# One core, long convolution and gated feed-forward: a new order of work, batched reciprocal roots, residual through the matmul, first loads on SyncE

## The chip, the cores and the metric

One core of a Trainium2 chip runs the whole program. The metric is the device time of one execution in microseconds (us). The kernel before took 297.24 us, the median of 8 runs from 296.48 to 297.85. Engines: PE is TensorE, DVE is VectorE, ACT is ScalarE, POOL is GpSimd, SP is SyncE, which here only issues DMAs.

## The reference, cut to what matters

```python
def _A_ref(q, k, v, shift_k, ssm_k, ssm_D):          # S = 2048, D = 640, 4 taps
    k_shift = sum of k_pad[:, t:t + S, :] * shift_k[:, ks - 1 - t]
    kv = k_shift * v
    y = irfft(rfft(kv, 2 * S) * rfft(ssm_k, 2 * S))[:S]   # long causal convolution
    y = y + kv * ssm_D
    return q * y

def _B_ref(x, w_gate, w_up, w_down):                 # F = 1728
    return (silu(x @ w_gate) * (x @ w_up)) @ w_down

x = A_q
h = x + _A_ref(_layernorm(x), A_k, A_v, A_shift_k, A_ssm_k, A_ssm_D)
h2 = h + _B_ref(_layernorm(h), B_w_gate, B_w_up, B_w_down)
```

The layernorm divides by the root of the variance plus 1e-5 and has no learned scale. All inputs and the output are bf16.

## The kernel before, in words

The 2048 rows are cut into 4 blocks n of 512 rows, and a block into 4 tiles q of 128 rows. The long convolution is done by blocks: each block of kv and each block of the convolution kernel is transformed by matmuls with cosine and sine matrices of length 1024, the transforms are multiplied elementwise and summed for every pair of blocks that adds to an output block, and a matmul brings the sum back.

The stages, with their lines in the kernel before:

- *Kernel blocks* (`gload`, `g_transform`): ssm_k block p is brought in transposed, blocks 0 and 1 by PE transposes (L334) and a copy on ACT (L338), blocks 2 and 3 by a transposing DMA (L323). It is then transformed by PE (L361) and copied to SBUF by ACT (L364).
- *kv* (`front_first` for block 0, `front_tile` for the others): block 0 multiplies k by the four taps on DVE (L395) and shifts by matmuls with banded matrices out of `perm` (L405); the other blocks load k four times, shifted, and do it on DVE (L378 to L381). `front` then folds each block into a sum and a difference of its halves, one half mirrored (L429 to L433), so that the transforms are half as long.
- *x transform* (L443, copies L448), *products* (`pair`, L453: each pair is 8 or 6 elementwise operations of 2,560 elements per partition on DVE).
- *Inverse* (`inverse`): matmuls with WI (L550), copies on ACT (L554), the mirrored half by matmuls with a flip matrix (L574), multiplication by the layernormed q (L566, L567, L577), the sum into x (L578), the second layernorm, and a transposing DMA of the result into hT (L582).
- *Layernorm* (`ln`, `scale`): per tile ACT makes the mean (L520) and the sum of squares (L521); POOL makes the variance plus eps (L524) and raises it to the power -0.5 (L525), on one column each; DVE scales the tile (L532), into xln for the first layernorm and into hl for the second. The second layernorm of block 0 takes its statistics on DVE (L516, L517).
- *Feed-forward* (`ffn`): 14 chunks c of 128 columns (the last has 64) of gate and up by PE (L618), SiLU and a copy on ACT (L623, L630), their product on DVE into tT (L632), which is the condition for ACT to write sg and uc again and so for PE's two psF buffers; then four down tiles of 28 matmuls (L644) whose last chunk uses 64 rows, the residual added on DVE from PSUM (L652), and a store by SP.

The order of the work is not written out. Every operation is handed to a planner (`Plan.add`) with its engine, an assumed duration, a priority `pr`, an earliest time `t0`, and what it reads and writes. `Plan.order` places the operations one by one, per engine, the ready one with the best priority, and repeats this up to `ROUNDS` times with priorities from a pass backwards. The result is one fixed list per engine, and each engine works its list in order. `psA` and `psF` are two PSUM tiles each; front, x transform and inverse use psA, kernel transforms and feed-forward psF. DMAs are issued by SP's list and, at the start, ACT's. At the start ACT's list loads the taps (wrow), v of block 0, perm, ssm_D, and later WG, WX, x of block 0 and WI; SP's loads k of block 0, then ssm_k blocks 0 and 1.

Of the kernel before, what the change touches and what calls it, by code (L numbers as in the profile page):

```python
# [16 lines left out]
D = 640  # L17
# [37 lines left out]
class Plan:  # L55
# [3 lines left out]
    def __init__(self, pools):  # L59
        self.ops, self.writer, self.readers = [], {}, {}  # L60
        self.pools, self.held = pools, {}

    def add(self, eng, dur, fn, r=(), w=(), pr=0, acq=None, rel=None, kb=0, after=(), t0=0.0):
        deps = set()
        for k in r:
            if k in self.writer:
                deps.add(self.writer[k])
        for k in list(w) + list(after):
            if k in self.writer:
                deps.add(self.writer[k])  # L70
            deps |= self.readers.get(k, set())
        i = len(self.ops)
        self.ops.append(dict(eng=eng, dur=dur, fn=fn, deps=deps, pr=pr, acq=acq and acq[0], rel=rel and rel[0], group=(acq or rel or (0, 0))[1], kb=kb, w=list(w), t0=t0))
        for k in r:
            self.readers.setdefault(k, set()).add(i)
        for k in w:
            self.writer[k], self.readers[k] = i, set()
        return i
# [42 lines left out]
    def forward(self, rank):  # L121
# [15 lines left out]
        while len(out) < n:  # L137
# [44 lines left out]
            for u in users[i]:  # L182
                lag = LAG.get(e, 0.12) if ops[u]["eng"] != e or o["kb"] else 0.12 if e == "DVE" else 0.0
                at[u] = max(at[u], done + lag)
# [6 lines left out]
ROUNDS = 3  # L191
# [3 lines left out]
MOVE = "add"  # L195
RES, XACT, VEC, TRANS = (), (), True, {2: 28, 3: 28}
# [11 lines left out]
def kernel(  # L208
# [33 lines left out]
    WI_h = nc.inline_tensor(make_basis()[2], name="const_wi")  # L242
    J_h = nc.inline_tensor(make_flip(), name="const_flip")
# [16 lines left out]
    kch = [tT[:, 2560 * i:2560 * (i + 1)].rearrange("p (a b) -> p a b", a=5) for i in range(2)]  # L260
# [9 lines left out]
    xln = [tl(f"xln{i}", [P, D]) for i in range(2)]  # L270
# [3 lines left out]
    y = [tl(f"y{i}", [P, D]) for i in range(2)]  # L274
    hl = [tl(f"hl{i}", [P, D]) for i in range(2)]
    drow = xln[0][0:1, :]
# [5 lines left out]
    junk = tl("junk", [P, D])  # L282
    mhalf = tl("mhalf", [P, 1], FP32)
    bn = [tl(f"bn{i}", [P, 2, 6], FP32) for i in range(2)]
    sm = {}
    smt = tl("sm", [P, NB * 8, 8], FP32)
    for n in range(NB):
        for q in range(4):
            for s in (1, 2):
                sm[n, q, s] = smt[:, 8 * n + 2 * q + s - 1, :]  # L290

    WG = last[:].rearrange("p a b -> p (a b)")[:, 0:4096].rearrange("p (a b) -> p a b", a=4)
    gT = [wd[:, 0:4, :], wd[:, 4:8, :], wd[:, 8:12, :], hT[1][:].rearrange("p a b -> p (a b)").rearrange("p (a b) -> p a b", a=4)]

# [14 lines left out]

    def load(q, dst, src, w, pr, kb, r=(), dur=0.45, after=(), t0=0.0):  # L310
        eng = {"SP": nc.sync, "ACT": nc.scalar, "POOL": nc.gpsimd}[q]
        add(q, dur, lambda: eng.dma_start(out=dst, in_=src), r=r, w=w, pr=pr, kb=kb, after=after, t0=t0)


    add("POOL", 0.1, lambda: nc.gpsimd.memset(ones[:], 1.0), w=["ones"], pr=-99)
    add("POOL", 0.1, lambda: nc.gpsimd.memset(mhalf[:], -0.5), w=["mhalf"], pr=-9)
    load("ACT", wrow, A_shift_k.partition_broadcast(1).rearrange("o a b -> o (a b)"), ["wrow"], -100, 5)
    add("ACT", 1.5, lambda: nc.scalar.activation(sg[0][0:1, 0:P], ones[:], ACT.Silu), r=["ones"], w=["sg0"], pr=-50)
    load("ACT", drow, A_ssm_D.partition_broadcast(1), ["drow"], -95.5, 5)

    def gload(p, pr, q="SP"):
# [5 lines left out]
        for kt in range(4):  # L327
            g = ("F", "T", p, kt)

            def mm(g=g, kt=kt):  # L330
# [6 lines left out]
            add("PE", 0.45, mm, r=["flip", f"kch{p % 2}"] + (["drow"] if p == 0 and kt == 0 else []), w=[g], pr=pr + 50, acq=("F", g))  # L337
            add("ACT", act(D), lambda g=g, kt=kt: nc.scalar.copy(gT[p][:, kt, :], ps(g).rearrange("p a b -> p (a b)")[:, 0:D]),  # L338
                r=[g], w=[f"gT{p}"], pr=pr - 40, rel=("F", g))
# [11 lines left out]
    for t in range(4):  # L351
        wcast(t)

    def g_transform(p, pr):
        for ct in range(NCT):
            g = ("F", "G", p, ct)

            def mm(g=g, ct=ct):
                for kt in range(4):
                    for h in range(2):  # L360
                        nc.tensor.matmul(ps(g)[:, h, 0:NH], WG[:, kt, ct * P:(ct + 1) * P],  # L361
                                         gT[p][:, kt, h * NH:(h + 1) * NH], start=(kt == 0), stop=(kt == 3))
            add("PE", 8 * 0.137, mm, r=["WG0", "WG1", f"gT{p}"], w=[g], pr=pr, acq=("F", g))
            add("ACT", act(D), lambda g=g, ct=ct: nc.scalar.copy(r3(G[p][ct // 4][:, ct % 4, :]), ps(g)[:, :, 0:NH]),  # L364
                r=[g], w=[Gk[p] + "cs"[ct // 4]], pr=pr - 900, rel=("F", g))
# [4 lines left out]

    def front_tile(n, q, pr):
# [7 lines left out]
        add("DVE", dve(2 * D), lambda: nc.vector.tensor_add(kd[:, 0:2, :], kd[:, 0:2, :], kd[:, 2:4, :]), r=ks, w=[kn], pr=pr)  # L379
# [7 lines left out]
    def first_loads():  # L387
        load("SP", kfirst[:], kk[0:MB, :].rearrange("(m p) d -> p m d", p=P), ["x1_0", "x1_1", "x1_2", "x1_3"], -98, 640)
        load("ACT", hT[0][:].rearrange("p a b -> p (a b)").rearrange("p (a b) -> p a b", a=4), vv[0:MB, :].rearrange("(m p) d -> p m d", p=P), ["v0all"], -96, 640)
        load("ACT", WG, WG_h.ap(), ["WG0", "WG1"], -95, 1024)  # L390

    def front_first(q, pr):
# [15 lines left out]
        if turn:  # L408
# [6 lines left out]
            add("ACT", act(D), lambda: nc.scalar.copy(r3(y[q][:]), ps(gv)[:, :, 0:NH]), r=[gv], w=[f"y{q}"], pr=pr - 60, rel=("F", gv))  # L415
            add("DVE", dve(D, True), lambda: nc.vector.tensor_mul(r3(rev[:, m, :]), ps(g)[:, :, 0:NH], r3(y[q][:])), r=[g, f"y{q}"], w=["rev"], pr=pr, rel=("A", g))
        else:
            add("DVE", dve(D, True), lambda: nc.vector.tensor_mul(r3(kv[:, q, :]), ps(g)[:, :, 0:NH], r3(v)), r=[g, "v0all"], w=[f"kv{q}"], pr=pr, rel=("A", g))

    def front(n, pr):  # L420
# [13 lines left out]

    def x_transform(n, pr):
# [20 lines left out]

    def hbuild(p, pr):
# [3 lines left out]

    def pair(j, p, pr, how):
# [43 lines left out]
    def ln(n, q, which, pr, vec=False, t0=0.0):  # L506

        s, k, src = sm[n, q, which], f"sm{n}{q}{which}", xin[n % 2][:, q, :]
        xk = f"x{n % 2}_{q}"
        e = nc.gpsimd  # L510
        if vec:
# [6 lines left out]
            add("DVE", 1.1, bns, r=[xk], w=[k + "a", f"bn{q % 2}"], pr=pr)  # L518
        else:
            add("ACT", act(D) + 0.25, lambda: nc.scalar.activation(junk[:], src, ACT.Copy, scale=-1.0 / D, accum_out=s[:, 0:1]), r=[xk], w=[k + "a"], pr=pr, t0=t0)  # L520
            add("ACT", act(D) + 0.45, lambda: nc.scalar.activation(junk[:], src, ACT.Square, bias=s[:, 0:1], accum_out=s[:, 1:2]), r=[xk, k + "a"], w=[k + "b"], pr=pr)  # L521

        def fin():
            e.tensor_scalar(s[:, 3:4], s[:, 1:2], 1.0 if vec else 1.0 / D, EPS, op0=ALU.mult, op1=ALU.add)  # L524
            e.tensor_tensor(s[:, 4:5], s[:, 3:4], mhalf[:], op=ALU.pow)  # L525
            if which == 1 and n in XACT:
                e.tensor_tensor(s[:, 5:6], s[:, 0:1], s[:, 4:5], op=ALU.mult)
        add("POOL", 1.5 + 0.7 * (which == 1 and n in XACT), fin, r=[k + "a", k + "b"], w=[k], pr=pr)

    def scale(dst, n, q, which):  # L530
        s = sm[n, q, which]
        nc.vector.tensor_scalar(dst, xin[n % 2][:, q, :], s[:, 0:1], s[:, 4:5],  # L532
                                op0=ALU.subtract if (n, which) == (0, 2) and VEC else ALU.add, op1=ALU.mult)

    def load_x(n, pr, queue="SP"):
        load(queue, xin[n % 2][:], xq[n * MB:(n + 1) * MB, :].rearrange("(m p) d -> p m d", p=P), [f"x{n % 2}_{q}" for q in range(4)], pr, 640, t0=(14, 30, 0, 0)[n])
        for q in range(4):
            ln(n, q, 1, pr + 30, t0=(26, 50, 0, 0)[n])

    def inverse(n, pr):  # L540
        a, ak = A[n], Ak[n]
        x, b = xin[n % 2], n % 2
        for m in range(2):
# [11 lines left out]
            for half in (0, 1):  # L555
                q = 2 + m if half == 0 else 1 - m
                yb, yk, lk = y[half], f"y{half}", f"xln{half}"
                xk = f"x{b}_{q}"
                s = sm[n, q, 1]
                if n in XACT:  # L560
                    add("ACT", act(D), lambda q=q, half=half, s=s: nc.scalar.activation(xln[half][:], x[:, q, :], ACT.Identity, scale=s[:, 4:5], bias=s[:, 5:6]),
                        r=[f"sm{n}{q}1", xk], w=[lk], pr=pr)
# [166 lines left out]
```

## Time and profile before

| what | value |
|---|---|
| median of the runs | 297.24 us |
| the profiled execution | 297.03 us |
| its span, first to last instruction | 295.2 us |
| ACT, largest groups | SiLU L623 x56 33.7 us; copies L630 x56 33.1; squares L521 x28 23.7; kernel transform copies L364 x32 21.8; means L520 x28 20.9 |
| POOL | L525 x32 35.1 us, mean 1,097 ns; L524 x32 30.7 us, mean 960 ns |
| DVE, products L453 | 115 us in 78 operations of about 1,480 ns each |
| PE, largest groups | L618 133.8 us in 540 matmuls; L644 64.8 us in 448; L361 37.6 us in 256 |
| DMA | 44.13 MB, mean 149 GB/s |

The busy times of PE are those of single matmuls and overlap; the time from start to start is shorter than the duration. The granted clock of TensorE was 0.999 of full speed over the span. A row of the timeline has the start, the length, engine, line, operation, operands, the count, and in brackets the idle time of the engine before it and what ended it. In the chain of waits each piece is what the next one waited for.

### The profile page before, as it was taken

The numbers are of one execution on the slowest core, as the hardware profiler recorded it, in microseconds if no ns is written. First come the engines' busy times: TensorE is split into PE (matmuls) and PEld (weight loads), VectorE is DVE, ScalarE is ACT, GpSimd is POOL, SyncE is SP. The second block draws the span as 40 slices with busy tenths as digits, with TensorE's granted clock in tenths as the row PEclk, the third lists the DMA queues.
The fourth block names the chain that finished last, engine by engine and source line by source line (L and its number), as shares of the span: only waits on it lengthen the run. The fifth ranks groups of instructions, "written<-read, shape, count | busy, mean of one in ns | idle before, by whom it ended". The sixth has DMA issues, their size and how long they took to land.

```text
span 295.2 us, 4406 instructions
## 1 busy us (share of the span) xinstructions
PE 275.5 (93%) x1651; PEld 157.9 (53%) x1651; DVE 229.7 (78%) x301; ACT 169.6 (57%) x323; POOL 66.2 (22%) x70
## 2 busy tenths in 40 slices
PE   3598959999999989999999999999998999999995
PEld 1266737666645535564545565555445665444563
DVE  0559797999999999999999999999999931211211
ACT  5117895898856589004996790169955732555300
POOL 0000262395000056000362174008800220000000
PEclk9999999999999999999999999999999999999999
DMA  7982399508635677934676394163654151654011
GB/s 230 392 270 88 119 238 348 121 2 245 212 91 131 178 234 160 258 131 115 169 230 206 65 192 95 44 200 91 152 130 102 42 127 54 174 139 110 0 47 46
DMA packets 67898, 44.13 MB, mean 149 GB/s; under 512 B 25442, under 2 KB 65955, under 8 KB 67748
## 3 DMA queue, kind: packets, MB, share of 16 engines
q1 hardware_dynamic: 66240, 40.23, 49.8%
q10 hardware_dynamic: 1636, 3.61, 3.4%
q8 instruction: 13, 0.21, 0.3%
q14 instruction: 9, 0.07, 0.1%
HBM read 37.28 MB, written 2.62 MB: 135 GB/s over the span
## 4 chain that ended last, share of the span: by engine, by line
DVE 52%; PE 30%; issue 5%; DMA 4%; ACT 4%; POOL 3%; ACTq 0%; DVEq 0%
DVE s L453 20%; DVE T L453 13%; PE psF L644 11%; PE psF L618 10%; DVE tT L632 3%; DVE k L378 3%; DMA perm<-const_flip 3%; PE psA L405 3%; POOL sm L525 2%; DVE k L379 2%; PE psF L361 2%; PE psA L550 2%; PE psA L443 2%; DMA hT<-hl 1%; DVE o L652 1%
## 5 line engine op out<-in xcount | busy, mean ns | idle before, releaser
L618 PE MATMUL psF<-hT,wg 128*128 128x512 bf16 x280 | 69.4, 379 | 0.8 <-ACT uc L630 0.8
L524 POOL TENSOR_SCALAR sm<-sm 128x1 f32<-128x1 f32 x32 | 30.7, 960 | 169.9 <-ACT junk L521 159.4
L644 PE MATMUL psF<-wd,tT 128*128 128x320 bf16 x448 | 64.8, 299 | 1.1 <-DVE tT L632 0.9
L618 PE MATMUL psF<-hT,wu 128*128 128x512 bf16 x260 | 64.4, 379 | 0.4 <-DMA wu<-in_B_w_up_dram 0.4
L623 ACT ACTIVATE sg<-psF 128x512 bf16<-128x512 f32 (+1 forms) x56 | 33.7, 602 | 45.7 <-PE psF L618 36.4
L644 PEld LDWEIGHTS <-tT 128*128 128x128 bf16 x448 | 41.4, 97 | 24.1 <-issue 6.9
L453 DVE TENSOR_TENSOR T<-s,s 128x2560 bf16<-128x2560 bf16 x32 | 47.2, 1481 | 0.0
L453 DVE TENSOR_TENSOR s<-s,T 128x2560 bf16<-128x2560 bf16 x32 | 47.1, 1481 | 0.0
L618 PEld LDWEIGHTS <-wg 128*128 128x128 bf16 x280 | 27.2, 98 | 32.7 <-issue 2.3
L630 ACT CAST uc<-psF 128x512 bf16<-128x512 f32 (+1 forms) x56 | 33.1, 591 | 15.8 <-PE psF L618 15.6
L632 DVE TENSOR_TENSOR tT<-sg,uc 128x512 bf16<-128x512 bf16 (+1 forms) x56 | 23.2, 418 | 24.4 <-ACT uc L630 24.4
L618 PEld LDWEIGHTS <-wu 128*128 128x128 bf16 x260 | 25.4, 98 | 29.5 <-DMA wu<-in_B_w_up_dram 0.8
L525 POOL TENSOR_TENSOR sm<-sm,mhalf 128x1 f32<-128x1 f32 x32 | 35.1, 1097 | 2.7
L361 PEld LDWEIGHTS <-s 128*128 128x128 bf16 x256 | 25.0, 98 | 11.8 <-issue 2.1
L361 PE MATMUL psF<-wd,s 128*128 128x320 bf16 x192 | 28.4, 299 | 0.9 <-ACT wd L338 0.5
L652 DVE TENSOR_TENSOR o<-psF,x 128x640 bf16<-128x640 f32 x16 | 13.1, 817 | 19.3 <-PE psF L644 19.3
L364 ACT CAST s<-psF 128x640 bf16<-128x640 f32 x32 | 21.8, 693 | 7.7 <-PE psF L361 7.6
L521 ACT ACTIVATE junk<-x,sm 128x640 bf16<-128x640 bf16 x28 | 23.7, 846 | 0.3
L520 ACT ACTIVATE junk<-x 128x640 bf16<-128x640 bf16 x28 | 20.9, 745 | 3.7 <-DVE x L578 2.9
L550 PE MATMUL psA<-s,WI 128*128 128x320 bf16 x128 | 18.9, 299 | 2.9 <-DVE s L453 2.8
L453 DVE TENSOR_TENSOR s<-s,s 128x2560 bf16<-128x2560 bf16 x14 | 20.5, 1479 | 1.2 <-ACT s L364 1.2
L443 PE MATMUL psA<-kv,WX 128*128 128x320 bf16 x128 | 20.5, 299 | 0.0
(55 smaller groups left out, 231.7 us busy)
## 6 DMA issues: line engine op xcount, KB each, us to landing
k<-in_A_k_dram SPq DMA_DIRECT2D x12, 640.0 KB, 4.8
wg<-in_B_w_gate_dram SPq DMA_DIRECT2D x24, 320.0 KB, 3.2
wu<-in_B_w_up_dram SPq DMA_DIRECT2D x24, 320.0 KB, 3.7
out_dram<-o SPq DMA_DIRECT2D x16, 160.0 KB, 1.9
wd<-in_B_w_down_dram SPq DMA_DIRECT2D x1, 2080.0 KB, 10.6
v<-in_A_v_dram SPq DMA_DIRECT2D x12, 160.0 KB, 4.7
x<-in_A_q_dram SPq DMA_DIRECT2D x3, 640.0 KB, 5.3
tT<-in_A_ssm_k_dram SPq DMA_DIRECT2D x2, 640.0 KB, 10.1
```

The costliest lines, as they stand in the source:

```text
L361: nc.tensor.matmul(ps(g)[:, h, 0:NH], WG[:, kt, ct * P:(ct + 1) * P], gT[p][:, kt, h * NH:(h + 1) * NH], start=(kt == 0), stop=(kt == 3))
L443: nc.tensor.matmul(ps(g)[:, h, 0:NH], WX[:, kt, ct * P:(ct + 1) * P], kv[:, base + kt, h * NH:(h + 1) * NH], start=(kt == 0), stop=(kt == 1))
L453: add("DVE", dve(n * D), lambda: f(o, a, b), r=ks(ak) + ks(bk), w=ks(ok), after=["WG0", "WG1"] if ok[:2] == "s7" else [], pr=pr)
L521: add("ACT", act(D) + 0.45, lambda: nc.scalar.activation(junk[:], src, ACT.Square, bias=s[:, 0:1], accum_out=s[:, 1:2]), r=[xk, k + "a"], ...
L524: e.tensor_scalar(s[:, 3:4], s[:, 1:2], 1.0 if vec else 1.0 / D, EPS, op0=ALU.mult, op1=ALU.add)
L525: e.tensor_tensor(s[:, 4:5], s[:, 3:4], mhalf[:], op=ALU.pow)
L550: nc.tensor.matmul(ps(g)[:, h, 0:NH], WI[:, 4 * part + ct, m * P:(m + 1) * P], a[part][:, ct, h * NH:(h + 1) * NH], start=(ct == 0), stop= ...
L618: i = nc.tensor.matmul(ps(gr)[:, which, :], w[:, kt, cc * P:(cc + 1) * P], hT[b][:, kt, :], start=(kt == 0), stop=(kt == 4))
L623: apart(gr, 0, nc.scalar.activation(sg[s][:z, :], ps(gr)[:z, 0, :], ACT.Silu))
L630: add("ACT", act(MB), lambda gr=gr, s=s, z=z, merged=merged: nc.scalar.copy(uc[s][:z, :], ps(gr)[64:128, 0, :] if merged else ps(gr)[:, 1, ...
L632: add("DVE", dve(MB), lambda c=c, s=s, z=z: TM(tT[:z, c * MB:(c + 1) * MB], sg[s][:z, :], uc[s][:z, :]), r=[f"sg{s}", f"uc{s}"], w=[f"tT{c ...
L644: nc.tensor.matmul(ps(gr)[:, h, 0:NH], tT[:z, c * MB + m * P:c * MB + (m + 1) * P], wd[:z, c, h * NH:(h + 1) * NH], start=(c == 0 and n no ...
```

## The change

It has these parts. The function names are those of the diff.

1. *Order.* `ROUNDS` is 0: one pass of the planner, whose priorities are shifted per stage by a table (`URGENCY`) and whose starts are held back by another (`EARLIEST`); a decorator gives each stage its name. All four engines' lists differ from before nearly everywhere.
2. *Loads.* v of block 0, ssm_D, WX, x of block 0 and WI move from ACT's list to SP's; ACT keeps the taps, perm and WG. In the list that results SP begins with one ssm_k block (block 1), then k and v of block 0, ssm_D, WX, ssm_k block 0, x of block 0, WI and then k and v of block 1. wd, before one load of 2,080 KB and one of 80, becomes five, each issued after a tT chunk is written.
3. *Warm-up.* Eight matmuls of 512 columns on zeros, five at the very start and three after the tap broadcast.
4. *Layernorm.* ACT also makes variance times 1/D plus eps (a third ACT operation on one column); POOL does a single power, for 1, 2 or 4 tiles at once (15 operations in place of 64); ahead of a batch DVE does a small `tensor_reduce` over 96 elements (`port`, 11 in all), nine of them reading the tile that ACT's Square writes; for the first layernorms of blocks 1 to 3 DVE also copies one element of the power's result (`idle`), and so waits for it.
5. *First scale of blocks 1 to 3* on ACT (12 tiles; a one-column operation for the bias and the scale itself) in place of DVE.
6. *Residual* of blocks 0 to 2: two matmuls of 320 columns with the identity per down tile, then a copy on ACT in place of DVE's add. Block 3 keeps the add.
7. *Down matmuls* use 128 rows for the last chunk as well; the unused rows of tT and wd are set to zero once.

Parts that other settings of the same code could use (rows fetched by index, a transposed way back, DMA accumulation) are switched off by `HOW = 'JJJJ'`, `TURN`, `ACC` and `MOVES`.

```diff
-        i = len(self.ops)
+        i, pr = len(self.ops), pr + URGENCY.get(self.stage or "none", 0)
+        t0 = max(t0, EARLIEST.get(self.stage or "none", 0))
...
-ROUNDS = 3
+ROUNDS = 0
-RES, XACT, VEC, TRANS = (), (), True, {2: 28, 3: 28}
+RES = (0, 1, 2)
+XACT = [(n, 1) for n in (1, 2, 3)]
+VEC = (0,)
+SPAN = 96
+HOW = 'JJJJ'
+TRANS = {2: 28, 3: 28}
+WARM = (0.43, 5, 3)
...
+    add("DVE", 0.35, lambda: nc.vector.memset(junk[:], 0.0), w=["hl0"], pr=-999)
+    add("DVE", 0.35, lambda: nc.vector.memset(tT[64:128, 13 * MB:], 0.0), w=["tz"], pr=-998)
+    add("DVE", 0.35, lambda: nc.vector.memset(wd[64:128, 13, :], 0.0), w=["wz"], pr=-998)
+    def warm(name, n, pr, r=()):
+        g = ("F", name)
+        def mm():
+            for i in range(n):
+                nc.tensor.matmul(ps(g)[:, i % 2, :], junk[:, 0:P], junk[:, 0:MB], start=True, stop=True)
...
-    load("ACT", drow, A_ssm_D.partition_broadcast(1), ["drow"], -95.5, 5)
+    load("SP", drow, A_ssm_D.partition_broadcast(1), ["drow"], -95.5, 5)
...
+            def spread():
+                nc.scalar.activation(junks[j][:], src, ACT.Square, bias=s[:, 0:1], accum_out=s[:, 1:2])
+                nc.scalar.activation(var[:, c:c + 1], s[:, 1:2], ACT.Identity, scale=1.0 / D, bias=eps[:])
+    def port(key, deps, pr, lag, src=None):
+        src = still if src is None else src
+        add("DVE", 0.06 + SPAN / 960, lambda: nc.vector.tensor_reduce(idle[:], src[:, 0:SPAN], axis=mybir.AxisListType.X, op=ALU.add), r=deps, w=[key], pr=pr, lag=lag)
+    def root(n, qs, which, pr):
+        cs, vec = sorted(column(n, q, which) for q in qs), which == 2 and n in VEC
+        gap, gk, lag = (still, "flip", 0.3) if vec else (junks[qs[-1] % 2], f"junk{qs[-1] % 2}", 0.0)
...
+        if n < NB - 1 or which == 1:
+            gkey = [ks[0] + "g"]
+            port(gkey[0], deps + [gk], pr - 20000, lag, gap)
+        add("POOL", 0.8, lambda: nc.gpsimd.tensor_tensor(rstd[:, c0:c1], var[:, c0:c1], mhalf[:, 0:c1 - c0], op=ALU.pow), r=deps + gkey, w=ks, pr=pr)
+        if (n, which) in XACT:
+            add("DVE", 0.08, lambda: nc.vector.tensor_copy(idle[:], rstd[:, c0:c0 + 1]), r=ks, w=[ks[0] + "h"], pr=pr - 20000)
...
+        def on_act():
+            nc.scalar.activation(s[:, 2:3], s[:, 0:1], ACT.Copy, scale=r)
+            nc.scalar.activation(dst, src, ACT.Identity, scale=r, bias=s[:, 2:3])
...
-                        z = 64 if c == 13 else P
                         for h in range(2):
-                            nc.tensor.matmul(ps(gr)[:, h, 0:NH], tT[:z, c * MB + m * P:c * MB + (m + 1) * P],
-                                             wd[:z, c, h * NH:(h + 1) * NH], start=(c == 0 and n not in RES), stop=(c == 13))
+                            nc.tensor.matmul(ps(gr)[:, h, 0:NH], tT[:, c * MB + m * P:c * MB + (m + 1) * P],
+                                             wd[:, c, h * NH:(h + 1) * NH], start=(c == 0 and not res), stop=(c == 13))
...
-    load_x(0, -10, "ACT")
+    load_x(0, -10, "SP")
-    load("ACT", WI[:], WI_h.ap(), ["WI"], -5, 512, t0=16)
+    load("SP", WI[:], WI_h.ap(), ["WI"], -5, 512, t0=16)
...
+            load("SP", wd[:, c0:c1, :], B_w_down[c0 * P:c1 * P, :].rearrange("(kt p) d -> p kt d", p=P), [f"wd{i}"], 1200, 160 * (c1 - c0),
+                 r=[f"tT{2 * min(i, 2) + 1}"], after=["gT0", "gT1", "gT2"])
```

## The prediction

> **What bounds it.** I read the page from the shares down to the chain, then the chain's last part, then VectorE's and PE's rows in order of time. First the page: busy shares, the 40 slices, the chain by engine.
>
> ```profile
> PE 275.5 (93%) x1651; PEld 157.9 (53%) x1651; DVE 229.7 (78%) x301; ACT 169.6 (57%) x323; POOL 66.2 (22%) x70
> PE   3598959999999989999999999999998999999995
> DVE  0559797999999999999999999999999931211211
> DVE 52%; PE 30%; issue 5%; DMA 4%; ACT 4%; POOL 3%; ACTq 0%; DVEq 0%
> ```
>
> VectorE (DVE) is full from about 24 us to 227 us and nearly idle afterwards; PE is full throughout. The chain agrees: DVE carries it first, PE at the end. The end of that chain, in order of time (start, length):
>
> ```profile
> 225.51 1.49 DVE s L453
> 227.04 2.35 PE psA L550 x16
> 231.56 14.86 PE psF L644 x104
> 246.42 29.24 PE psF L618 x135
> 275.67 15.96 PE psF L644 x112
> 291.65 0.82 DVE o L652
> ```
>
> So the span is two halves joined at the last product of block 3: DVE must reach it (226.9), then PE runs 64.6 us from 227.04 to 291.65 without a gap, then 3.55 us to the end of the span, 295.2. The execution was 297.03, that is 1.83 outside the span; the median of the runs shown is 297.24, 0.2 above it.
>
> PE busy overstates PE's work. Back-to-back starts are 0.2166 us for 512 columns (29.24/135) and 0.1365 for 320 (L361, 8 in 1.09). With these the program holds 267 us of PE work, and PE between 44.2 and 227.0 is idle only 6.9 us. Two nearly full engines feed each other; DVE is the one that is waited for, by some 7 us.
>
> **The start.** The timeline's first rows:
>
> ```profile
> 7.28 2.89 DVE L395 TENSOR_TENSOR k<-x,w 128x2560 bf16<-128x2560 bf16 x2 [7.28 <-ACT w L349]
> 10.93 2.32 PE L405 MATMUL psA<-k,perm 128*128 128x320 bf16 x8 [4.42 <-DMA perm<-const_flip]
> 34.27 1.49 DVE L453 TENSOR_TENSOR s<-s,s 128x2560 bf16<-128x2560 bf16 x1 [1.19 <-ACT s L364]
> 42.67 2.89 DVE L453 TENSOR_TENSOR s<-s,T 128x2560 bf16<-128x2560 bf16 x2
> ```
>
> perm, behind 640 KB of v on ACT's queue, starts PE; pair(0,0), the first product stage, begins at 34.27 and ends at 45.45.
>
> After: perm is ACT's second load, and SP brings ssm_k (640 KB), then k, then v. By the windows the transfers moved 1.9 MB by 8 us, 2.7 by 10; k had landed at 5.4, and ACT's queue got about 28% of the bytes (its v, 640 KB, landed at 9.9). So k, now 1,280 KB down SP's queue, lands when about 1,780 KB have moved: 7.9 us. The last w4 copy now waits for a transpose of ssm_k, about 7.7. DVE starts at 8.0 instead of 7.28, and the k product that PE wants first is DVE's second: 8.0+2.9 = 10.9, as before. PE is then no longer at half pace (2.32 us for 8 matmuls, later 1.09 for 8), and 20 of the 40 ssm_k transposes are behind it. The x0, WX and WI loads now queue on SP ahead of k's next rows, which wait for PE to free k4 at about 16 and land at about 21, just when DVE wants them.
>
> Following PE, ACT and DVE by these durations: the first difference of kv and rev (L432 before) comes at 20.6 instead of 22.7, kernel transform 0 is copied out at 36.7 instead of 34.2, since ACT now does block 0's first layernorm between those copies (12 us of ACT work from 24 us), and pair(0,0) ends at 42.8 instead of 45.45. It runs unbroken, as the k tiles that were inside it come later. Ends: 40.5 (k at 6) to 46 (k or x0 3 us late).
>
> **DVE up to the last product.** Starts are 1.40 us apart for 2,560 elements, 0.74 for 1,280 or 640 from PSUM, 0.40 for 640, 0.36 for a scale.
>
> ```profile
> L652 DVE TENSOR_TENSOR o<-psF,x 128x640 bf16<-128x640 f32 x16 | 13.1, 817 | 19.3 <-PE psF L644 19.3
> L532 DVE TENSOR_SCALAR xln<-x,sm 128x640 bf16<-128x640 bf16 x16 | 6.7, 438 | 0.0
> L516 DVE BATCH_NORM_STATS2 bn<-x 128x6 f32<-128x320 bf16 x8 | 3.4, 469 | 0.0
> ```
>
> Removed ahead of the mark: 8 residual adds x 0.74 = 5.9 (blocks 0 and 1; block 2's lie after it) and 8 scales x 0.36 = 2.9. Added: 11 tensor_reduces of 96 elements, 3 tiny copies, 4 one-column ops, 3 memsets. No such reduce is in the trace; by BN_STATS (469 ns for 320[...]) one costs 0.1 to 0.25, I take 0.16: 1.8. The rest about 1.35. Net -5.7: 208.4 to 202.7 us of work, of which 28.4 lie before pair(0,0)'s end (29.2 before). To do after it: 174.3, against 179.2 that took 181.45.
>
> Here a rule speaks against two edits. The Trainium skill, "VectorE: DVE Perf Modes", Rules for kernel authors, calls tensor_reduce the slowest op of the engine and would restructure it; by that the gates are a plain loss of 1.8. "ScalarE: Activation LUTs", Rules for kernel authors, says multiply and add belong on VectorE. The rows: a 640-element scale is 0.36 on DVE and 0.58 plus about 0.2 for the bias column on ACT. By the rule the 12 moved scales lose 12 x 0.42 = 5; by this profile they gain 12 x 0.36 on the engine that is waited for, ACT being 57% busy. I take the profile, with one reserve: in the 21.7 us of PE work behind inverse 1, ACT's list becomes 22 us (9 SiLUs and copies 8.7, layernorm 8, scales 3, copies out 2.6), without a margin.
>
> **Waits: the gates.** The pow on GpSimd in order of time, beside DVE's wait for it:
>
> ```profile
> 52.34 0.55 POOL L525 TENSOR_TENSOR sm<-sm,mhalf 128x1 f32<-128x1 f32 x1
> 109.91 3.51 POOL L525 TENSOR_TENSOR sm<-sm,mhalf 128x1 f32<-128x1 f32 x1
> 113.45 0.45 DVE L532 TENSOR_SCALAR hl<-x,sm 128x640 bf16<-128x640 bf16 x1 [0.44 <-POOL sm L525]
> ```
>
> 0.55 beside BN_STATS, 3.51 behind a row of TENSOR_TENSORs, ended only by DVE's own idleness. The change puts a reduce in front of each batch. Nine of the eleven read what ACT's Square writes, so DVE, in order, stands at them until that Square is done, and everything behind it (products, and tT which frees PE's buffers) stands too. Three tiny copies make DVE wait for the pow itself. Costs: a gate from 0 to a whole Square, 0.83; most are placed when ACT should be through, so 0.15 x 9 = 1.4. A hold-out 0 to 0.55; half: 0.8. The two waits of 0.44 go: -0.9. The old waits of 2.3 stay, and I add 1.1 since PE is now only some 5 us ahead. Together 4.7, against 2.3 (ends 1 and 11).
>
> Last product: 42.8+174.3+4.7 = 221.8 instead of 226.9.
>
> **PE after it.** In both programs inverse 3's second half, down 2, all of ffn 3 and down 3 follow. Added: 8 residual matmuls of block 2, 8 x 0.137 = 1.1. Removed: something the loads show.
>
> ```profile
> 279.12 0.11 PEld L644 LDWEIGHTS <-tT 64*128 64x128 bf16 x2 [0.26 <-issue]
> 279.50 0.79 PEld L644 LDWEIGHTS <-tT 128*128 128x128 bf16 x7 [0.26 <-issue]
> ```
>
> A down tile of 28 matmuls takes 4.01 us (DVE's o at 279.61, 283.62, 287.63), where 28 x 0.1365 = 3.82; the load pauses on entering and leaving the 64-row chunk. The change pads it to 128 rows of zeros: -0.19 x 8 tiles = -1.5. Thus 64.6+1.1-1.5 = 64.2.
>
> Down 2 hides block 3's layernorm and transposes: from inverse 3's second half to ffn 3 PE had 19.3 us, now about 20. The last layernorm square of block 3 ended 11.45 us after 227.04; it now has four ACT scales (two of them late, 1.7), a column op per tile (0.8) and two output copies (1.2) in front: about 15. The pow, the scale and a transpose (2.6 to landing) end at 19.5. Slack falls from 3 us to 0.5; I charge 0.5, ends 0 and 3.
>
> End: 221.8+0.14+64.2+0.5+3.55 = 290.2, plus 1.83: **292.0**, against 297.03.
>
> **At nothing.** Output stores stay on SP; the output copies of blocks 0 to 2 lie beside DVE-limited stretches. wd comes in five pieces, each waiting for a tT: the next weight loads stand behind it on SP, but their buffer frees about 6 us before PE needs them and they land in 3.2 to 3.7; uncovered, 0 to 1 us. The memsets and eight warm matmuls lie in the empty first 8 us.
>
> **Rivals.** *The waits dissolve.* The order leaves DVE nearly stall-free (1 us) and PE sets the pace: PE stands at 28.5 us of its work at 36.7, and 207.8 at the inverse: 215.9 plus about 2.5 of waiting. 218.4+64.2+0.5+3.55+1.83 = 288.5. For it: PE's 7 us of slack; against: DVE's 217 even without stalls.
>
> *The gates stall DVE.* Behind each inverse, ACT is full, its Square late, and DVE stands at the gate for the whole 0.83: 9 x 0.83 + 3 x 0.55 = 9.1 instead of 2.2, so 298.9: slower. It decides from a mean wait of about 0.7 us a gate. For it: ACT's 22 in 21.7; against: before, ACT caught up in each such stretch.
>
> *The gates don't open.* The reduce is too short, the pow waits as before, the hl scales wait: +1.5, 293.5.
>
> *The first loads are late.* k or x0 3 us late, all of it on the path: 295.
>
> **How the numbers follow.** Forecast 0.48, waits dissolve 0.18, gates stall 0.22, gates don't open 0.06, loads late 0.06. The forecast's own range is 290 to 295; to leave no more than 0.2 outside I go from 287.5 to 298.5. No change, within 0.2% of 297.24 (what a measurement of this kernel can tell), is 296.6 to 297.8: 0.05, out of the upper edge of the forecast and the lower of the stalled case. Slower is most of the stalled case and 0.03 of the others' edges, 0.23; faster 0.72.
>
> **What would show it.** Right: last product at 220 to 223, pair(0,0) ended by 43.5, down tiles at 3.82 us (4.09 with residual), pows near 0.55. Wrong: reduces with idle time on ACT Squares above 0.5 us each, DVE's first product after 10 us, or PE idle ahead of ffn 3 on the transposes.

## The result and the profile after

The changed kernel takes **294.42 us** (median of 22 runs, 292.89 to 296.53) against 297.04 for the kernel before in the same comparison: ratio **0.991, 95% interval 0.9896 to 0.9924**. It is faster, by 2.6 us where 5.0 were forecast. The profiled execution took 293.57 us, its span is 291.8, at full clock. Ratios and their intervals leave out executions more than 1.5% above the fastest of the same kernel; the medians count all.

The page of the changed kernel: busy shares, two rows of the 40 slices, the chain by engine.

```profile
PE 279.3 (96%) x1683; PEld 164.5 (56%) x1683; DVE 220.4 (76%) x300; ACT 197.5 (68%) x387; POOL 20.2 (7%) x22
...
PE   7698999979999998999999999999999999999995
...
DVE  1466799999999989999999999999997710121212
...
PE 43%; DVE 41%; DMA 7%; SPq 3%; issue 3%; ACT 1%; DVEq 0%
```

DVE lost 9 us of work and POOL 46; ACT gained 28. The chain has moved: PE carried 30% of it and DVE 52%, now they are level, and DMA and SP's queue have 10% between them, most of it ahead of pair(0,0). DVE's timeline there (start, length; in brackets the idle time before and what ended it):

```profile
10.99 1.49 DVE L460 TENSOR_TENSOR s<-x,w 128x2560 bf16<-128x2560 bf16 x1 [7.24 <-DMA x<-in_A_k_dram]
...
24.57 0.82 DVE L483 TENSOR_TENSOR kv<-psA,hT 128x640 bf16<-128x640 f32 x1 [2.88 <-PE psA L470]
...
38.33 1.48 DVE L520 TENSOR_TENSOR s<-s,s 128x2560 bf16<-128x2560 bf16 x1
...
44.65 2.89 DVE L520 TENSOR_TENSOR s<-s,T 128x2560 bf16<-128x2560 bf16 x2
```

The first product waits for k until 10.99; before, it started at 7.28, when the taps had been copied. pair(0,0) ends at 47.46, 2 us later than before. The end of the chain, in order of time:

```profile
197.26 21.58 PE psF L762 x100
218.85 2.17 PE psA L674 x16
221.02 3.24 PE psF L762 x15
224.26 2.17 PE psA L674 x16
...
243.82 29.14 PE psF L762 x135
272.96 15.23 PE psF L793 x112
...
288.21 0.82 DVE o L801
```

The timeline there, DVE and then PE:

```profile
220.39 3.02 DVE L520 TENSOR_TENSOR s<-s,T 128x2560 bf16<-128x2560 bf16 x2
...
220.86 1.24 PE L762 MATMUL psF<-hT,wg 128*128 128x512 bf16 x5
221.94 1.24 PE L762 MATMUL psF<-hT,wu 128*128 128x512 bf16 x5
223.02 1.24 PE L762 MATMUL psF<-hT,wg 128*128 128x512 bf16 x5
224.10 2.34 PE L674 MATMUL psA<-s,WI 128*128 128x320 bf16 x16
```

A product counts as ended 1.40 us after its start, when DVE could start its next, as in the forecast. The last one starts at 221.92, so it ends at 223.3. The inverse that needs it (L674) starts only at 224.10 (the chain books it from 224.26): 15 feed-forward matmuls stand in front of it on PE, which has had no wait since 171.60. Before, the inverse followed the product by 0.14 us. So the difference of the two spans, 3.4 us, is made up as follows:

| stretch | before | after | difference |
|---|---|---|---|
| start to the end of pair(0,0) | 45.47 | 47.45 | +2.0 |
| from there to the end of the last product (DVE) | 181.4 | 175.9 | -5.6 |
| from there to PE's second half of the inverse | 0.14 | 0.78 | +0.6 |
| PE from there to its last matmul | 64.6 | 64.1 | -0.5 |
| PE's end to the span's end | 3.55 | 3.6 | 0 |

### The profile page after: what moved, and what is told of

The parts are those of the page before. It is cut to its first block, busy times and chain, and to the rows that moved or that the text cites. A ratio compares the mean times of both kernels' runs of the same rounds, so it can differ in the third digit from the quotient of the medians.

```text
span 291.8 us, 4484 instructions
## 1 busy us (share of the span) xinstructions
PE 279.3 (96%) x1683; PEld 164.5 (56%) x1683; DVE 220.4 (76%) x300; ACT 197.5 (68%) x387; POOL 20.2 (7%) x22
## 3 DMA queue, kind: packets, MB, share of 16 engines
q10 hardware_dynamic: 290, 1.25, 1.1%
## 4 chain that ended last, share of the span: by engine, by line
PE 43%; DVE 41%; DMA 7%; SPq 3%; issue 3%; ACT 1%; DVEq 0%
PE psF L762 20%; PE psF L793 16%; DVE s L520 13%; DVE T L520 9%; DVE k L438 4%; DMA x<-in_A_k_dram 3%; DVE tT L776 3%; SPq L380 3%; PE psA L470 2%; DMA k<-in_A_k_dram 2%; DMA wg<-in_B_w_gate_dram 2%; DVE k L443 2%; PE psA L674 1%; PE psA L510 1%; DVE kv L445 1%
## 5 line engine op out<-in xcount | busy, mean ns | idle before, releaser
L762 PE MATMUL psF<-hT,wu 128*128 128x512 bf16 x260 | 64.6, 379 | 0.0
L793 PE MATMUL psF<-wd,tT 128*128 128x320 bf16 x448 | 63.5, 299 | 0.0
L793 PEld LDWEIGHTS <-tT 128*128 128x128 bf16 x448 | 43.8, 98 | 17.2
L774 ACT CAST uc<-psF 128x512 bf16<-128x512 f32 (+1 forms) x56 | 32.5, 580 | 15.2 <-PE psF L762 15.2
L627 POOL TENSOR_TENSOR rstd<-var,mhalf 128x2 f32<-128x2 f32 (+2 forms) x15 | 19.7, 1314 | 218.4 <-ACT var L608 215.8
L607 ACT ACTIVATE junk<-x,sm 128x640 uint8<-128x640 bf16 x28 | 23.4, 834 | 0.3
L799 ACT CAST o<-psF 128x640 bf16<-128x640 f32 x12 | 8.3, 688 | 22.4 <-PE psF L793 22.4
L604 ACT ACTIVATE junk<-x 128x640 uint8<-128x640 bf16 x28 | 20.6, 737 | 0.2 <-DMA x<-in_A_q_dram 0.2
L520 DVE TENSOR_TENSOR s<-s,s 128x2560 bf16<-128x2560 bf16 x14 | 20.6, 1481 | 0.0
L515 ACT CAST s<-psA 128x640 bf16<-128x640 f32 x29 | 19.0, 698 | 0.0
L674 PE MATMUL psA<-s,WI 128*128 128x320 bf16 x128 | 18.7, 299 | 0.1
```

Source lines behind the costliest of these rows:

```text
L520: add("DVE", dve(n * D), lambda: f(o, a, b), r=ks(ak) + ks(bk), w=ks(ok), after=["WG0", "WG1"] if ok[:2] == "s7" else [], pr=pr)
L604: add("ACT", 0.74, lambda: nc.scalar.activation(junks[j][:], src, ACT.Copy, scale=-1.0 / D, accum_out=s[:, 0:1]), r=[xk], w=[k + "a", f"ju ...
L607: nc.scalar.activation(junks[j][:], src, ACT.Square, bias=s[:, 0:1], accum_out=s[:, 1:2])
L674: nc.tensor.matmul(ps(g)[:, h, 0:NH], WI[:, 4 * part + ct, m * P:(m + 1) * P], a[part][:, ct, h * NH:(h + 1) * NH], start=(ct == 0), stop= ...
L762: i = nc.tensor.matmul(ps(gr)[:, which, :], w[:, kt, cc * P:(cc + 1) * P], hT[b][:, kt, :], start=(kt == 0), stop=(kt == 4))
L774: add("ACT", act(MB), lambda gr=gr, s=s, z=z, merged=merged: nc.scalar.copy(uc[s][:z, :], ps(gr)[64:128, 0, :] if merged else ps(gr)[:, 1, ...
```

## The experiments

Twelve kernels ran. In all but one (the planner's own order) every operation keeps the place that the order of the changed kernel, or of the kernel before, gives it, and only what the diff shows is moved or exchanged. The diffs of this part are shortened. Ratios are to the kernel before, timed beside each set; the changed kernel's is 0.991, and a difference from it in us is that of the two ratios times 297. The stretches as above, from each profile:

| kernel | ratio (95%) | first product | pair(0,0) ends | last product ends | PE from there to its end |
|---|---|---|---|---|---|
| before | 1 | 7.28 | 45.47 | 226.9 | 64.7 |
| changed | 0.991 (0.9896 to 0.9924) | 10.99 | 47.45 | 223.3 | 64.9 |
| WG behind v | 0.9816 (0.9774 to 0.9858) | 8.44 | 45.27 | 220.7 | 65.0 |
| k and v ahead of ssm_k | 0.9968 (0.993 to 1.0005) | 7.08 | 50.58 | 227.8 | 65.0 |
| the same, more warm matmuls | 0.9986 (0.9955 to 1.0016) | 7.08 | 52.09 | 228.3 | 64.9 |
| no gates | 1.0065 (1.0039 to 1.0091) | 10.86 | 47.23 | 228.4 | 65.0 |
| scales back on DVE | 0.9968 (0.9944 to 0.9991) | 11.0 | 47.56 | 226.1 | 64.3 |
| residual back on DVE | 1.0056 (1.0026 to 1.0087) | 11.05 | 47.99 | 230.5 | 63.8 |
| the planner's own order | 0.9979 (0.9958 to 0.9999) | 7.08 | 46.25 | 224.1 | 66.2 |
| last chunk of 64 rows again | 0.9961 (0.9936 to 0.9985) | 11.2 | 47.60 | 225.1 | 66.7 |
| before, with 128 rows | 0.9976 (0.9956 to 0.9997) | 7.27 | 46.13 | 227.7 | 63.1 |
| block 2's residual on DVE | 0.9856 (0.9819 to 0.9893) | 11.0 | 47.62 | 223.3 | 63.9 |
| WG behind v and that | 0.9791 (0.9762 to 0.9821) | 8.52 | 45.82 | 221.6 | 64.1 |
| and with three gates only | **0.9764** (0.974 to 0.9789) | 8.51 | 44.88 | 222.0 | 63.6 |

### The start: WG behind v

```diff
-    load("ACT", WG, ...)               # third on ACT's queue, issued at 1.70
+    nc.sync.dma_start(out=WG, ...)     # on SP, behind v, issued at 2.34
```

> The changed kernel with one load moved: WG (1 MB, first used by PE at 25.6 us) is issued on SP behind v instead of on ACT's queue at 1.70 us. Theory A (the start is on the path, and k is late because WG shares the engines with it): k lands at about 8 instead of 10.9, DVE's first product starts near 8.3, pair(0,0) ends near 45 instead of 47.46, and the end comes 1.5 to 2.7 us earlier: ratio to before about 0.983 to 0.986 instead of 0.991. Rival B (PE's transforms or ACT's copies set pair(0,0)'s date): the first product moves to about 8, but pair(0,0) still ends at 47 and the ratio stays at 0.991. Rival C (the queues' share is not what delays k): k lands at 10 to 11 as before.

Measured: 291.29 us. Its first product and pair(0,0):

```profile
8.44 1.49 DVE L460 TENSOR_TENSOR s<-x,w 128x2560 bf16<-128x2560 bf16 x1 [4.69 <-DMA x<-in_A_k_dram]
...
36.15 1.49 DVE L520 TENSOR_TENSOR s<-s,s 128x2560 bf16<-128x2560 bf16 x1
...
42.47 2.89 DVE L520 TENSOR_TENSOR s<-s,T 128x2560 bf16<-128x2560 bf16 x2
```

The product starts 2.55 us earlier, pair(0,0) ends 2.2 earlier and the last product 2.7: the start is on the path, nearly in full, and one load of 1 MB in the wrong place cost the change as much as its whole measured gain. B and C fall; the ratio lies a little below what A expected.

### The start: k and v ahead of ssm_k

```
 SP:   k, v, ssm_k       (was ssm_k, k, v)
 PE:   last tap, warm, V0, conv 0, V1, conv 1, four transposes   (were: one ahead of the last tap, three ahead of V0)
 ACT:  last tap, y0, y1, four copies out of the transposes
```

> The changed kernel with SP's first three loads in the order k, v, ssm_k instead of ssm_k, k, v, and the four transposes of that ssm_k block and their copies moved behind block 0's second convolution on PE and ACT, so that the last tap copy no longer stands behind a transpose. WG stays where it was. Theory A (start on the path): k lands at about 6, the first product starts when w4 is complete, at 7 to 8, v at about 11, pair(0,0) ends 2 to 3 us earlier, ratio to before 0.981 to 0.986. Rival B (PE's transforms set pair(0,0)'s date): the four transposes, 3 us of PE at half pace, only move to a later place where PE has no gap, pair(0,0) ends at 46.5 to 48 and the ratio is 0.989 to 0.993.

Measured: 297.79 us, slower than the changed kernel, though the first product started at 7.08. Two rows of the 40 slices, PE's timeline around the last convolution with DVE's wait for it, then the row of one window (start and end, length, busy times of PE, PEld, DVE, ACT and POOL, the granted clock, the DMA share and GB/s):

```profile
PE   8679999989999998999999889999999999999995
...
PEclk9986999999999999999999999999999999999999
```

```profile
21.07 0.27 PE L391 MATMUL psF<-perm,tT 128*128 128x128 bf16 x1 [0.50 <-ACT wd L395]
...
23.73 3.93 PE L470 MATMUL psA<-s,perm 128*128 128x320 bf16 x14
...
27.69 0.82 DVE L483 TENSOR_TENSOR kv<-psA,hT 128x640 bf16<-128x640 f32 x1 [9.19 <-PE psA L470]
```

```profile
20.70:27.50 6.80, 6.43 (x30) 3.57 (x30) 0.00 (x0) 4.09 (x9) 0.00 (x0) 0.50 1.09 230
```

Fourteen matmuls of the last convolution take 3.93 us where the changed kernel's take 2.06: the granted clock is half from 20.7 to 27.5. DVE waits 9.19 us for the result (2.88 in the changed kernel); for the first 5.2 of them PE is still at the transposes (17.41 to 23.73), in part at the cut clock. In nine of the twelve runs, the profiled one among them, the mean clock was 0.986 to 0.989; the two at 1.000 took 293.8 and 293.9 us, a ratio of 0.989, about what B expected. So the clock costs some 4 us, and the transposes that now stand between the convolutions presumably take back the rest of what the early k gives; there is no profile of a run at full clock that would show it. A is not refuted by this, but it doesn't carry: an early first product is worth something only if what follows it on PE keeps pace.

I then tried to name the cause of the cut: PE idles 2.49 us ahead of v in this order, so I filled that gap.

```diff
-            for i in range(n):
+            for i in range(n if name == "a" else 9):
```

> The kernel with k and v ahead of ssm_k, with nine instead of three warm matmuls behind the last tap matmul, which fill PE's idle 2.5 us ahead of v. Theory C (that kernel is slow because the clock is cut after PE's gaps: granted clock 0.88 between 20 and 47.5 us): the clock stays at 1.0 there, pair(0,0) ends at 45 to 47, ratio 0.983 to 0.990. Rival D (it is slow because the four transposes and their copies now stand in PE's and ACT's way between the convolutions): pair(0,0) still ends after 47 at full clock, ratio 0.990 to 0.996. Rival G (the cut has another cause): the clock is cut as before, ratio about 0.997.

Measured: 297.61 us, the clock again at half, from 22.5 to 29.3 us, nine of twelve runs again at 0.987 or 0.988, the two at 1.000 at 294.4 and 294.7. The gap ahead of v is not the cause, so C's remedy fails, and G holds. At full clock the two runs have ratios of 0.990, where the ranges of C and D meet, so between these two nothing is decided. What cuts the clock stays open. Both kernels have in common the transposes with waits of 0.5 to 0.8 us for ACT between them, just ahead of the cut; that this is the cause was not tried alone.

### The gates left out

```diff
-        nc.vector.tensor_reduce(idle[:], src[:, 0:SPAN], ...)    # 11 of them
-        nc.vector.tensor_copy(idle[:], rstd[:, c0:c0 + 1])       # 3 of them
```

> The changed kernel in the same order, with none of the eleven tensor_reduces ahead of the rstd batches and none of the three one-element copies behind them: the pows start as soon as their variances are there. The gates cost DVE about 11 x 0.16 + 3 x 0.1 = 2.1 us. Theory P (they pay: a pow beside DVE's two-input products is stretched to several us and its readers wait): pows of 2 to 5 us, waits of DVE or ACT for rstd of 0.5 to 3 us at three or more of the scales, last product no earlier than 223, ratio 0.991 to 1.000. Rival Q (the readers come late enough anyway): the last product comes 1 to 2 us earlier, the end by at most 1 us since PE is nearly full, ratio 0.987 to 0.990.

Measured: 299.33 us, 4.6 more than the changed kernel and outside both ranges. The place, first in the changed kernel, POOL, DVE and ACT in order of time:

```profile
154.34 1.52 POOL L627 TENSOR_TENSOR rstd<-var,mhalf 128x4 f32<-128x4 f32 x1 [35.94 <-ACT var L608]
...
154.92 0.23 DVE L614 TENSOR_REDUCE idle<-junk 128x1 f32<-128x96 uint8 x1
...
155.89 0.30 ACT L636 ACTIVATE sm<-sm,rstd 128x1 f32<-128x1 f32 x1 [0.21 <-POOL rstd L627]
...
156.48 0.13 DVE L629 COPY idle<-rstd 128x1 f32<-128x1 f32 x1
```

and without gates:

```profile
153.94 6.85 POOL L627 TENSOR_TENSOR rstd<-var,mhalf 128x4 f32<-128x4 f32 x1 [33.93 <-ACT var L608]
...
160.83 0.29 ACT L636 ACTIVATE sm<-sm,rstd 128x1 f32<-128x1 f32 x1 [5.15 <-POOL rstd L627]
...
162.70 3.77 PE L674 MATMUL psA<-s,WI 128*128 128x320 bf16 x16 [2.43 <-ACT es L678]
...
164.89 0.43 DVE L776 TENSOR_TENSOR tT<-sg,uc 128x512 bf16<-128x512 bf16 x1 [4.97 <-ACT uc L774]
```

Beside a row of two-input products on DVE the pow of four columns takes 6.85 us instead of 1.52; it ends 0.9 us after DVE has fallen idle (its last product there ends at 159.9). DVE doesn't read it soon; the reader is ACT, which since the change does the scale, and ACT is in order: behind its scale stand es and uc. PE waits for es, DVE for uc, 4.97 us. PE then starts again at a lower pace: 16 matmuls in 3.77 us, where it had needed 2.33 for its previous 16, at half the granted clock from 163.4 to 166.8. That cut is not the loss: three of the twelve runs had a mean clock of 1.000 and took 299.1 to 300.0 us. The last product comes 5.1 us later; the one wait behind the long pow, through ACT, is 4.97 of DVE's time. The hl scales, read by DVE, lost only 0.60 and 0.59, and the work of the gates that is saved about makes up for these.

### Block 2's residual, and two edits together

```diff
-            four output copies on ACT, 8 identity matmuls     # block 2
+            TA(r3(ot[s][:]), ps(gr)[:, :, 0:NH], r3(xin[b][:, m, :]))     # block 2, on DVE
```

> The changed kernel in the same order, with block 2's residual back on DVE (four adds from PSUM in place of ACT's four output copies, and the 8 residual matmuls of block 2 left out); blocks 0 and 1 stay on PE. Theory T (PE alone carries the last 64 us): those 8 matmuls are 8 x 0.137 = 1.1 us on the path, the end comes 1.0 to 1.2 us earlier, ratio about 0.987. Rival U (DVE's adds, 0.8 us each, delay block 3's layernorm and its transposes, so PE waits ahead of ffn 3): nothing gained or up to 1 us lost, ratio 0.990 to 0.994.

Measured: 292.82 us, PE's stretch behind the last product 63.9 instead of 64.9. T holds: in the last 64 us DVE has time for the adds, and PE has none for eight matmuls.

With WG behind v as well:

> The changed kernel with WG behind v on SP and block 2's residual on DVE. Alone they gave 0.9816 and 0.9856 against 0.991. If they add (one moves the last product, the other shortens what PE does behind it): pair(0,0) ends at 45.3, the last product at 220.5, PE's work behind it 64.1, the end at about 288.2, ratio 0.976 to 0.979. If PE, late at the last product, takes part of it back: 0.980 to 0.983.

Measured: 291.15 us, ratio 0.9791, just above the first range. That the two edits add isn't shown, since WG behind v alone had 291.29. In this profile PE's stretch behind the last product is 0.9 us shorter than with WG behind v alone, but pair(0,0) ended 0.55 us later.

### Three gates only

```diff
-            port(gkey[0], deps + [gk], pr - 20000, lag, gap)
+            port(gkey[0], deps + [gk], pr - 20000, lag, gap, which == 1 and n > 0)   # else no instruction
```

> The kernel with both (WG behind v on SP, block 2's residual on DVE) without eight of the eleven tensor_reduces: only those of the first layernorm of blocks 1 to 3 stay, with their one-element copies. Without any, DVE waited 4.97 us for what stood behind the four-column pow of block 2's first layernorm and only 0.60 and 0.59 at two hl scales. Theory F (one gate pays, the others cost their 0.16 us each): DVE waits about 1.2 us at the hl scales and saves 1.3, the time is that of the kernel with both within 0.6 us. Rival A (each gate pays): slower than it by 1 us or more.

Measured: 290.81 us, against 291.15 with all eleven; the two aren't told apart. F holds, with waits of 0.59 us at each of two hl scales: the gates that pay are among those whose rstd ACT reads (this run doesn't separate the three), the other eight pay about what they cost. It has the lowest ratio of all, 2.4% under the kernel before, and is below the changed kernel with intervals that don't touch.

### The parts moved from DVE, put back

```diff
-        add(*(("ACT", act(D) + 0.22, on_act) if on else ...    # twelve scales
+        add(*(("ACT", act(D) + 0.22, on_dve) if on else ...    # place of the list kept, work on DVE
```

> The changed kernel in the same order, with the twelve scales of the first layernorm of blocks 1 to 3 back on DVE (one instruction each) instead of ACT. Eight of them lie ahead of the last product: 8 x 0.36 = 2.9 us of DVE work. Theory V (DVE still sets the last product): it comes 2 to 3 us later, less the 1 us by which PE is late there, so the end is 1.5 to 2.5 us later, ratio 0.996 to 1.000. Rival E (since the change PE sets the pace too): the end moves by less than 1 us, ratio 0.989 to 0.994.

Measured: 295.90 us, 1.7 more. The last product comes 2.8 us later, about the eight scales; PE's stretch is 0.6 shorter, since PE is no longer late (the inverse starts 0.19 us behind the product instead of 0.78). Theory V.

```diff
-            two identity matmuls per tile, nc.scalar.copy(...)                  # blocks 0 to 2
+            TA(r3(ot[s][:]), ps(gr)[:, :, 0:NH], r3(xin[b][:, m, :]))     # on DVE
```

> The changed kernel in the same order, with the residual of blocks 0 to 2 back on DVE (twelve adds from PSUM in place of the output copies on ACT and of 24 identity matmuls). DVE has 8 x 0.74 = 5.9 us more ahead of the last product, PE 2.2 us less there and 1.1 less behind it. Theory V (DVE sets the last product): it comes 5 to 6 us later; with about 1 us of PE's lateness and 1.1 us of the tail to set against it the end is 3 to 4 us later, ratio 1.001 to 1.005. Rival E (PE sets the pace): the end is 0 to 1.5 us later or earlier, ratio 0.986 to 0.996.

Measured: 298.50 us, 4.3 more, the last product 7.2 later: V again, and more than the 5.9 of work. Of the rest 0.5 had come by the end of pair(0,0) and 0.6 are longer waits of DVE. All ten runs had a mean clock of 0.993 or 0.994 (in the profile half clock from 202.3 to 205.7), and what that adds isn't separated. These two show DVE as the engine that sets the last product in the changed kernel, as before.

### The order

```diff
-URGENCY = {"ffn 1": 429, ...}   EARLIEST = {"front_tile 1 0": 24, ...}   ROUNDS = 0
+URGENCY = {}   EARLIEST = {}   ROUNDS = 3
```

> The changed kernel with the two tables of priorities and earliest dates emptied and the planner's three rounds of before restored: all parts of the change are kept but the order is the planner's own. Theory O (the fixed order is what keeps DVE free of waits): the gates stand at ACT's Squares and DVE waits 3 to 8 us more between pair(0,0) and the last product, which comes at 226 to 231; ratio to before 0.999 to 1.018. Rival W (the work taken off DVE and the padding carry the gain): last product at 222 to 225, ratio 0.989 to 0.996.

Measured: 296.38 us, between the two ranges, so 2.0 of the 2.6 us hang on the order; but not as theory O had it. The gates and the longest new wait in this kernel, by groups (busy, mean ns, then idle before):

```profile
L681 DVE TENSOR_TENSOR y<-es,os 128x640 bf16<-128x640 bf16 x8 | 3.9, 490 | 2.3 <-ACT os L674 2.3
...
L610 DVE TENSOR_REDUCE idle<-junk 128x1 f32<-128x96 uint8 x9 | 2.2, 246 | 0.0
```

No gate waits. DVE's stretch is 2.0 us longer (1.6 of it one wait for ACT's os right behind pair(0,0), where the kernel before waits 1.72), PE's is 1.3 longer, and the start is 1.2 shorter: its first product starts at 7.08.

### The 128-row chunk

```diff
-                        z = 64 if c == 13 else P        # before: 64 rows; changed: 128
```

> The changed kernel in the same order with the last chunk of the down matmuls back at 64 rows. Theory S (the 64-row chunk costs PE 0.19 us a tile): the last four tiles take 4.0 us instead of 3.80; the eight tiles behind the last product give 1.5 us, and the four of block 1, which PE reaches without slack, up to 0.8 more: end 1.5 to 2.3 us later, ratio 0.996 to 0.999. Rival N (in this order the pause is covered): tiles of 3.8, ratio 0.991.

> The kernel before in its own order, with nothing changed but the last chunk of the down matmuls: 128 rows, the upper 64 zero in both operands (two memsets at the start on GpSimd). Theory S (entering and leaving the 64-row chunk costs PE 0.19 us a tile, and only the eight tiles behind the last product count): down tiles of 3.82 us instead of 4.01, the end 8 x 0.19 = 1.5 us earlier, ratio 0.995. Rival N (the pause of the weight load is covered by the matmuls and the tile stays at 4.0 us): ratio 1.000. Rival M (PE is the bound in the middle too): all sixteen tiles count, ratio 0.990.

Measured: with 64 rows the changed kernel takes 296.98 us, 1.5 more by the ratios (2.6 by the medians); with 128 rows the kernel before takes 296.28, 0.7 less, with an interval from 0.1 to 1.3. The weight loads of the last tile but one, in the changed kernel with 64 rows:

```profile
283.67 3.37 PEld L794 LDWEIGHTS <-tT 128*128 128x128 bf16 x26 [0.26 <-issue]
287.31 0.11 PEld L794 LDWEIGHTS <-tT 64*128 64x128 bf16 x2 [0.26 <-issue]
287.68 3.38 PEld L794 LDWEIGHTS <-tT 128*128 128x128 bf16 x26 [0.26 <-issue]
```

Tiles start 4.01 us apart, against 3.80 with 128 rows in both kernels. In the profiles PE's work from the inverse on changes by 1.6 in both, as S says. In the kernel before part of it went at the start (pair(0,0) 0.65 later; I had put the two memsets on GpSimd ahead of everything, but that they are the reason was not tried). In the changed kernel the last product moves by 1.8 too, more than the 0.8 expected; that PE, dense from 171.60, makes block 1's tiles count would be the expected part of it, and the rest is not explained.

## Why the prediction was right, and where it was off

The forecast was 292.0 against 297.03, the execution 293.57 and the median 294.42: the sign, the likeliest case and the range held, the gain was half of the forecast. By its own sum, which is 1.6 short:

| term | predicted | measured | off |
|---|---|---|---|
| pair(0,0) ends | 42.8 | 47.45 | +4.7 |
| DVE work and stalls to the last product | 174.3 + 4.7 | 175.9 | -3.1 |
| handover, PE, hT | 0.14 + 64.2 + 0.5 | 0.78 + 64.1 + 0 | 0 |
| PE's end to the end of the execution | 3.55 + 1.83 | 3.6 + 1.77 | 0 |

**The failed step** is the landing of k: "k, now 1,280 KB down SP's queue, lands when about 1,780 KB have moved: 7.9 us". It rested on ACT's queue taking 28% of the bytes, as v had before, and on SP's queue bringing one load after the other. k landed at 10.9. By then the two queues had moved (packets, MB, share of the 16 engines; q1 is SP's, q10 ACT's):

```profile
q1 hardware_dynamic: 1554, 1.78, 51.0%
q10 hardware_dynamic: 290, 1.25, 28.5%
```

ACT's queue held a whole megabyte early: WG, issued at 1.70, took 9.0 us, and the queue had 41% of the bytes, 1.25 MB where the forecast's figures come to 0.5. SP's queue had brought 1.78 MB, though ssm_k and k together are 1.31: v and other loads issued behind k ran beside it. So k took 3.0 MB and not 1.8. The listed rival of late loads had the mechanism (k 3 us late, all of it on the path) at 0.06, and WG behind v showed it: 2.2 of the 4.7.

The other 2.5 remain in the kernel with WG behind v, where the product starts at 8.44, not far from the 8.0 of the forecast. PE was late there: the first convolution still ran at half pace (8 matmuls in 2.34 us, where I had counted on full), 15 small matmuls for the transposes stand ahead of the last one, and the first difference of kv and rev comes at 23.25 instead of 20.6. But the first product of pair(0,0) starts at 36.15, ahead of the 36.7 for which I had the copy of kernel transform 0, and 36.15 plus six products of 1.40 and two scales is 45.27. From 36.7 six products alone end at 45.1: if the first starts when that copy is through, as it did before (34.27 after 34.2), my 42.8 doesn't follow from my own date.

**The stalls.** I took 4.7 us; the stretch holds 1.6 beyond the work, 1.24 of it one wait for k. All nine gates on a Square together waited 0.2 us, where I had 1.4, and the hold-outs none, where I had 0.8: the order places them when ACT is through. The reduces cost what was estimated (0.16 apart). The rule of the Trainium skill, "VectorE: DVE Perf Modes", Rules for kernel authors, that speaks against tensor_reduce agrees with their price (0.16 us for 96 elements, 0.36 for a scale of 640) and doesn't decide here: the gates, some 1.8 us of work by the estimate, are worth 4.6.

**What the gates are worth** I had wrong the other way: the rival in which they don't open was +1.5, from the 3.51 us pow of before and hl scales on DVE. I left out that the change itself moves a reader of rstd to ACT, in front of es and uc. Measured without gates: +4.6, slower than before.

**The moved work.** The scales were 2.9 us by the row, and 2.8 in the last product; the profile was the right side to take against the rule of "ScalarE: Activation LUTs", Rules for kernel authors. The residual of blocks 0 and 1 was 5.9 by the row, 7.2 in the last product. The residual of block 2 was costed at 1.1 on the path; it is 1.1 in PE's own work (64.1 against 63.0 from the inverse on), 0.9 with the handover, and it is a plain loss, which the sum contained and I didn't draw as a conclusion. The padding was 1.5 behind the last product, and is.

**The handover.** "PE is now only some 5 us ahead" was still generous: PE has no slack at the last product and comes 0.6 later behind it than before. **hT:** ffn 3 didn't wait, the half microsecond wasn't needed.

So two errors of opposite sign hid each other, the late start (+4.7) and the missing stalls (-3.1); that the time stayed within the forecast's own 290 to 295 is in part luck. The case of the dissolved waits came true in DVE's stretch and the case of the late loads at the start; neither alone. The listed signs say the same: the down tiles came as forecast (3.80 us), but the last product just missed its dates (223.3), pair(0,0) missed them by 4 us, the pows took 0.54 to 5.23 us, and one sign of being wrong came true, the first product after 10 us.

## What to carry to other kernels

A queue's share of the bytes, read from one profile, is not a constant: before counting on a first load, add up everything that any queue has outstanding until then, and send what isn't needed soon behind it. When an operation moves to another in-order engine, the wait for its input moves too; cost that wait by what stands behind it there, not by the engine that had it. Where one engine sets the first part and another the end, cut the edit at the seam: off DVE ahead of the last product, off PE behind it.

Undoing the parts singly costs 4.6 (gates), 4.3 (residual), 2.0 (order), 1.7 (scales) and 1.5 us (rows), 14 in all, far more than the 2.6 of the whole, though the late start takes 2 back; so these sizes don't add. The likely reason, not tried by itself, is that in an order fitted to its parts taking one out also spoils the fit.

## What the hardware showed that I had not expected

- The granted clock was half for 6.8 us (20.7 to 27.5, and 22.5 to 29.3) in the profiles of the two kernels with k and v ahead of ssm_k, and the mean clock was as low in 9 of 12 runs of each; filling the idle 2.5 us of PE did not help, and the cause is open. In two other profiles it was half for 3.4 us, beginning 0.7 to 0.8 us after a wait of PE had ended: without gates (163.4 to 166.8, a wait of 2.43 us) and with the residual on DVE (202.3 to 205.7, a wait of 2.25). In the latter a wait of 2.08 us at 135 us was followed by no cut.
- A pow of four columns on GpSimd took 1.02 to 1.52 us in three batches of the changed kernel and 5.23 in the fourth, which begins at 208.82; its gate comes only at 218.10 and ACT reads it from 219.42 on, so it holds nobody up; without gates the last two took 6.85 and 7.31.
- Eight warm matmuls didn't bring the first convolution to full pace: 2.29 us for 8 matmuls after them, 2.32 before the change without them. Fourteen didn't either: 2.31 in the kernel with more warm matmuls.
